# Linear attention and an MLP mixer on one core: head pairs, batched evacuations, weights cast by DMA, and the next batch's attention traced into each mixer

## The chip, the cores and the metric

The kernel runs on one core of a Trainium2 chip. A time is device microseconds (us) from launch to end, the median of several executions. The "span" in a profile runs from the first to the last instruction of one profiled execution and is some 2 us shorter. Engines are named as in the profile: PE (TensorE matmuls), PEld (TensorE weight loads), DVE (VectorE), ACT (ScalarE), POOL (GpSimd), SP (SyncE, which issues most transfers). An execution is called slow when it is over 1.5% above the fastest of the same kernel; only fast ones are compared.

## The reference, cut to what matters

Four batches, eight heads, 768 positions, head dimension 64. Retention attention carries a 64x64 state along the sequence; its output of all heads, side by side, is `x` (768 x 512) and goes through a two-stage mixer.

```python
# attention, per head h (gamma depends on h)
state = gamma * state + outer(k[t], v[t])
y[t]  = scale * q[t] @ state
# mixer, per batch
h  = relu(x.T @ w_tok1) @ w_tok2          # over positions: 768 -> 256 -> 768
u  = x + h.T
h2 = relu(u @ w_ch1) @ w_ch2              # over channels: 512 -> 1536 -> 512
out = u + h2
```

The recurrence is computed in six chunks of 128 positions: within a chunk a masked 128x128 score matrix, between chunks the state.

## The kernel before

All weights come first, as float32, and ACT casts them. Then 192 chunks (4 x 8 x 6) run one after the other, each with its own small loads, its own copies out of PSUM, and the state carried from chunk to chunk. The mixers follow in program order.

```python
for dst, src in ((w_tok1_sb, moe_w_tok1), ...):          # all weights first
    for i, t in enumerate(dst):
        nc.sync.dma_start(out=stg, in_=src[i * P:(i + 1) * P, :])
        nc.scalar.copy(t, stg)
for b in range(B):
    for h in range(H):
        for c in range(NC):
            ...                                          # three loads of 128 x 64
            nc.scalar.activation(qk16[:, :D], qk_sb[:, :D], AF.Copy, bias=0.0, scale=gt1p[h])
            nc.scalar.copy(k16, qk_sb[:, D:])
            nc.vector.tensor_scalar(vg16, v_sb, gk[h], None, ALU.mult)
            if c > 0:
                nc.scalar.copy(st16, st)
            nc.tensor.transpose(tp_ps, qk16, ident16)
            nc.scalar.copy(qgT, tp_ps[:D, :])
            nc.vector.tensor_copy(kT, tp_ps[D:, :])
            nc.tensor.matmul(a_ps, kT, qgT, start=True, stop=True)        # scores, 64 rows
            nc.vector.tensor_tensor(am_sb, a_ps, mask2[h], ALU.mult)
            nc.tensor.matmul(y_ps, am_sb, vg16, ...)
            nc.tensor.matmul(y_ps, qgT, st16, ...)
            nc.vector.tensor_copy(x_sb[b][c][:, h * D:(h + 1) * D], y_ps)
            nc.tensor.matmul(st_ps, k16, vg16, start=True, stop=True)
            nc.vector.tensor_scalar(st, st, g128[h], None, ALU.mult)
            nc.vector.tensor_tensor(st, st, st_ps, ALU.add)
# ... then, per batch, the mixer: 24 token matmuls of 512 columns, 24 transposes,
# 96 matmuls of 384 columns with w_ch1, 72 of 512 columns with w_ch2
```

## Time and profile before

| kernel before | value | where from |
|---|---|---|
| median time | 501.68 us (497.25 to 501.79, 3 runs) | times |
| span | 498.9 us | profile |
| first transpose, last transpose of attention | 21.0 and 446.7 us | the transposes' own list |
| PE, DVE, ACT, POOL busy | 75, 50, 56, 1% | first part of the page |
| mean granted clock | 0.832 | cores view |

The prediction below reads this profile part by part. The largest groups of instructions show many small ones. The columns are line, engine, operation, output and inputs, shapes and count, then busy time in us and the mean in ns, then the engine's idle time just before them and what ended most of it:

```profile
L120 ACT COPY qTt<-tp 64x128 f16<-64x128 f16 x192 | 49.7, 259 | 106.6 <-PE tp L117 103.1
L123 PE MATMUL p<-qTt,kTt 64*128 64x128 f16 x192 | 50.3, 262 | 38.5 <-DVE kTt L121 31.7
L125 DVE TENSOR_TENSOR am_sb<-p,dm 128x128 f16<-128x128 f32 x192 | 55.9, 291 | 45.3 <-PE p L123 36.3
```

Each of the three waits for another engine: that is the chain the prediction starts from.

### The profile page before, as it was taken

The numbers are of one execution on the slowest core, as the hardware profiler recorded it, in microseconds if no ns is written. First come the engines' busy times: TensorE is split into PE (matmuls) and PEld (weight loads), VectorE is DVE, ScalarE is ACT, GpSimd is POOL, SyncE is SP. The second block draws the span as 40 slices with busy tenths as digits, with TensorE's granted clock in tenths as the row PEclk, the third lists the DMA queues.
The fourth block names the chain that finished last, engine by engine and source line by source line (L and its number), as shares of the span: only waits on it lengthen the run. The fifth ranks groups of instructions, "written<-read, shape, count | busy, mean of one in ns | idle before, by whom it ended". The sixth has DMA issues, their size and how long they took to land.

```text
span 498.9 us, 7213 instructions
## 1 busy us (share of the span) xinstructions
PE 372.2 (75%) x1760; PEld 158.8 (32%) x1760; DVE 250.4 (50%) x1096; ACT 281.1 (56%) x1058; POOL 2.8 (1%) x15
## 2 busy tenths in 40 slices
PE   0034555547899999458999997568999998578997
PEld 0012222222344444222334433222344433222553
DVE  1035555555664566555744566554745566553012
ACT  6854444445787844456767744454677744456730
POOL 2000000000000000000000000000000000000000
PEclk9999999999957999655559998556758999557999
DMA  8832222222121232222211222222221233220002
GB/s 278 302 104 47 49 51 49 50 50 45 40 45 40 49 86 68 53 69 64 60 39 43 46 70 52 51 69 76 82 45 42 48 87 90 50 74 0 2 21 106
DMA packets 89899, 33.54 MB, mean 67 GB/s; under 512 B 83712, under 2 KB 84480, under 8 KB 89856
## 3 DMA queue, kind: packets, MB, share of 16 engines
q1 hardware_dynamic: 89856, 33.07, 25.1%
q8 instruction: 14, 0.23, 0.2%
q14 instruction: 29, 0.24, 0.2%
HBM read 26.74 MB, written 6.29 MB: 66 GB/s over the span
## 4 chain that ended last, share of the span: by engine, by line
PE 65%; DVE 14%; ACT 10%; DMA 5%; issue 5%; SPq 1%; ACTq 0%; DVEq 0%
PE acc L179 16%; PE acc L191 13%; PE p L123 8%; DVE am_sb L125 5%; PE p L131 5%; PE tp L117 5%; PE p L135 4%; PE p L130 4%; PE acc L152 4%; PE acc L162 3%; DVE kTt L121 3%; DMA wstg<-in_moe_w_ch_dram 3%; ACT qTt L120 3%; PE tp L173 2%; DVE x L132 2%
## 5 line engine op out<-in xcount | busy, mean ns | idle before, releaser
L120 ACT COPY qTt<-tp 64x128 f16<-64x128 f16 x192 | 49.7, 259 | 106.6 <-PE tp L117 103.1
L179 PE MATMUL acc<-uT,wc 128*128 128x384 f16 x384 | 95.2, 357 | 0.9 <-ACT h L185 0.4
L191 PE MATMUL acc<-wc,h 128*128 128x512 f16 x288 | 81.2, 389 | 0.1
L123 PE MATMUL p<-qTt,kTt 64*128 64x128 f16 x192 | 50.3, 262 | 38.5 <-DVE kTt L121 31.7
L125 DVE TENSOR_TENSOR am_sb<-p,dm 128x128 f16<-128x128 f32 x192 | 55.9, 291 | 45.3 <-PE p L123 36.3
L108 ACT ACTIVATE qk<-qk_sb,gt 128x64 f16<-128x64 f32 x192 | 66.5, 346 | 18.2 <-PE p L135 15.9
L132 DVE COPY x<-p 128x64 f32<-128x64 f32 x192 | 43.1, 225 | 66.0 <-PE p L131 54.5
L121 DVE COPY kTt<-tp 64x128 f16<-64x128 f16 x192 | 43.4, 226 | 48.5 <-ACT qTt L120 41.1
L117 PE MATMUL tp<-ident,qk 128*128 128x128 f16 x192 | 51.0, 266 | 22.4 <-ACT qk L110 22.1
L130 PE MATMUL p<-vg,am_sb 128*128 128x64 f16 x160 | 35.6, 222 | 29.3 <-DVE am_sb L125 29.2
L185 ACT ACTIVATE h<-acc 128x384 f16<-128x384 f32 x96 | 46.9, 489 | 17.9 <-PE acc L179 15.9
L111 DVE TENSOR_SCALAR vg<-v_sb,gk 128x64 f16<-128x64 f32 x192 | 46.9, 244 | 10.5 <-DMA v_sb<-in_v_dram 6.2
L123 PEld LDWEIGHTS <-kTt 64*128 64x128 f16 x192 | 18.7, 98 | 98.8 <-DVE kTt L121 80.6
L114 ACT CAST st<-state_sb 64x64 f16<-64x64 f32 x160 | 38.5, 241 | 17.5 <-DVE state_sb L140 15.3
L110 ACT CAST qk<-qk_sb 128x64 f16<-128x64 f32 x192 | 45.0, 234 | 0.9 <-DMA qk_sb<-in_k_dram 0.9
L135 PE MATMUL p<-vg,qk 128*64 128x64 f16 x160 | 35.3, 221 | 9.5 <-DVE x L132 4.7
L179 PEld LDWEIGHTS <-wc 128*128 128x128 f16 x384 | 33.2, 102 | 21.8 <-issue 6.9
L140 DVE TENSOR_TENSOR state_sb<-state_sb,p 64x64 f32<-64x64 f32 x128 | 27.3, 213 | 18.7 <-PE p L135 13.1
L131 PE MATMUL p<-st,qTt 64*128 64x64 f16 x160 | 34.9, 218 | 0.7 <-ACT st L114 0.6
L130 PEld LDWEIGHTS <-am_sb 128*128 128x128 f16 x160 | 16.7, 105 | 55.4 <-DVE am_sb L125 50.5
L198 DVE TENSOR_TENSOR o_sb<-x,acc 128x512 f32<-128x512 f32 x24 | 16.4, 685 | 35.6 <-PE acc L191 34.9
L135 PEld LDWEIGHTS <-qk 128*64 128x64 f16 x160 | 19.1, 120 | 44.0 <-issue 34.7
(35 smaller groups left out, 294.0 us busy)
## 6 DMA issues: line engine op xcount, KB each, us to landing
qk_sb<-in_q_dram SPq DMA_DIRECT2D x192, 32.0 KB, 1.7
qk_sb<-in_k_dram SPq DMA_DIRECT2D x192, 32.0 KB, 1.8
v_sb<-in_v_dram SPq DMA_DIRECT2D x192, 32.0 KB, 1.7
out_dram<-o_sb SPq DMA_DIRECT2D x24, 256.0 KB, 2.1
wstg<-in_moe_w_ch_dram SPq DMA_DIRECT2D x4, 768.0 KB, 8.8
wstg<-in_moe_w_ch_dram SPq DMA_DIRECT2D x12, 256.0 KB, 3.6
wstg<-in_moe_w_tok_dram SPq DMA_DIRECT2D x6, 128.0 KB, 2.3
wstg<-in_moe_w_tok_dram SPq DMA_DIRECT2D x2, 384.0 KB, 4.2
```

Source lines behind the costliest of these rows:

```text
L108: nc.scalar.activation(qk16[:, :D], qk_sb[:, :D], AF.Copy, bias=0.0, scale=gt1p[h])
L117: nc.tensor.transpose(tp_ps, qk16, ident16)
L120: nc.scalar.copy(qgT, tp_ps[:D, :])
L121: nc.vector.tensor_copy(kT, tp_ps[D:, :])
L123: nc.tensor.matmul(a_ps, kT, qgT, start=True, stop=True)
L125: nc.vector.tensor_tensor(am_sb, a_ps, mask2[h], ALU.mult)
L130: nc.tensor.matmul(y_ps, am_sb, vg16, start=True, stop=False)
L131: nc.tensor.matmul(y_ps, qgT, st16, start=False, stop=True)
L132: nc.vector.tensor_copy(x_sb[b][c][:, h * D:(h + 1) * D], y_ps)
L135: nc.tensor.matmul(st_ps, k16, vg16, start=True, stop=True)
L179: nc.tensor.matmul(h2_ps, w_ch1_sb[ct][:, ft * P:(ft + 1) * P], uT_sb[ct][:, sh * (S // 2):(sh + 1) * (S // 2)], start=(ct == 0), stop=(ct ...
L191: nc.tensor.matmul(o_ps, h2_sb[ft][:, i * P:(i + 1) * P], w_ch2_sb[ft], start=(ft == 0), stop=(ft == 11),)
```

## The change

Its intent: fewer and larger instructions beside the matmuls, no chain from chunk to chunk, no weight phase ahead of everything, and attention of batch b+1 laid among the mixer matmuls of batch b.

- Two heads share a tile of 128 partitions. Scores use 64 rows for each head; everything else uses the full array. The states of the two heads sit in a block-diagonal tile `R`, so one matmul reads both.
- The states of all chunks of a pair come from five matmuls and a short scan on DVE, not from a chain through the chunks. One copy empties three or six chunks.
- POOL casts k, scales the states and casts x and u to 16 bit.
- Weights are loaded by DMAs that POOL issues and that cast to 16 bit on the way, each issued behind the k cast of a pair.
- Attention is a generator of seven steps; the mixer loop advances it.

```diff
-            nc.sync.dma_start(out=stg, in_=src[i * P:(i + 1) * P, :])
-            nc.scalar.copy(t, stg)
+        if s == 0 and p == 2:
+            with tc.issue_after(kc.ins):
+                nc.gpsimd.dma_start(out=wc1, in_=moe_w_ch1.rearrange("(i p) j -> p i j", p=P))
...                                        # attention of one pair of heads
+        kc = nc.gpsimd.tensor_copy(k16..., kf...)            # 128 x 768
+        yield kc
+        for src, dst in ((q16, qT), (k16, kT)):
+            for c in range(NC):
+                nc.tensor.transpose(tp[:, c * P:(c + 1) * P], src[:, c]..., ident16)
+            nc.scalar.copy(dst, tp[:, :S])                   # six chunks at once
+        yield
+            for c in range(c0, c1):
+                nc.tensor.matmul(st[...], k16[:, c]..., v16[:, c]..., start=True, stop=True)
+            for c in range(c0, c1):                          # scan
+                    nc.vector.scalar_tensor_tensor(U[:, c], U[:, c - 1], gp[:, p:p + 1], s,
+                                                   ALU.mult, ALU.add)
+        for j in range(2):                                   # diagonal blocks of R
+            nc.gpsimd.tensor_scalar(R[r, :, r], U[r, :, r], g128[2 * p + j], None, ALU.mult)
+        yield
...                                        # scores and masks by three chunks, then y
+                    nc.tensor.matmul(o, qT[:, c * P:(c + 1) * P], R[:, c - 1], ...)
+                for j in range(2):
+                    nc.tensor.matmul(o[:, j * D:(j + 1) * D], ams[2 * hf + j][:, i], v16[:, c, j], ...)
+            nc.scalar.copy(xo, y...)
+            nc.gpsimd.tensor_copy(x16..., xo)
...                                        # the weave
+        for us in mlp(b):
+            spent += us
+            while steps and done < total and done < spent / MLP_US * total:
+                next(steps)                # one step of the next batch's attention
+                done += 1
```

## The prediction

> **What bounds the kernel now.** I read the busy shares first, then the table of busy time by stretches of 10 us, then the order of time of a single chunk, last the tail.
>
> ```profile
> PE 372.2 (75%) x1760; PEld 158.8 (32%) x1760; DVE 250.4 (50%) x1096; ACT 281.1 (56%) x1058; POOL 2.8 (1%) x15
> PE   0034555547899999458999997568999998578997
> ...
> PE 65%; DVE 14%; ACT 10%; DMA 5%; issue 5%; SPq 1%; ACTq 0%; DVEq 0%
> ```
>
> No engine is full. PE shows 75%, and 65% of the chain that ended last, but a matmul's recorded time is mostly its latency, so that row does not say PE is the limit. By stretches (start:end, length, then busy time and count of PE, PEld, DVE, ACT, POOL, granted clock, DMA share, GB/s):
>
> ```profile
> 10.00:20.00 10.00, 0.00 (x0) 0.00 (x0) 0.00 (x0) 9.73 (x23) 0.00 (x0) 1.00 0.87 342
> 60.00:70.00 10.00, 4.92 (x24) 2.33 (x23) 5.68 (x27) 4.50 (x21) 0.00 (x0) 1.00 0.22 48
> 170.00:180.00 10.00, 10.00 (x57) 4.38 (x58) 5.64 (x27) 6.46 (x25) 0.00 (x0) 1.00 0.23 52
> 210.00:220.00 10.00, 5.09 (x23) 2.46 (x23) 5.81 (x27) 4.58 (x22) 0.00 (x0) 0.50 0.20 44
> 470.00:480.00 10.00, 10.00 (x59) 5.47 (x57) 0.00 (x0) 7.07 (x15) 0.00 (x0) 1.00 0.00 0
> ```
>
> Until 20 us the core loads weights and ACT casts them; PE does nothing. In a stretch of attention alone (60 to 70) every engine is near half busy, which is the sign of a chain of waits. The mixer's dense matmuls (170 to 180) run *beside* attention, and DVE keeps its pace of 27 instructions per stretch: attention goes on at the same speed with or without the mixer. One chunk of one head in order of time:
>
> ```profile
> 63.90 0.29 PE L123 MATMUL p<-qTt,kTt 64*128 64x128 f16 x1 [0.36 <-DVE kTt L121]
> 64.23 0.29 DVE L125 TENSOR_TENSOR am_sb<-p,dm 128x128 f16<-128x128 f32 x1
> 64.58 0.23 PE L130 MATMUL p<-vg,am_sb 128*128 128x64 f16 x1 [0.39 <-DVE am_sb L125]
> 64.74 0.23 PE L131 MATMUL p<-st,qTt 64*128 64x64 f16 x1
> 65.01 0.23 DVE L132 COPY x<-p 128x64 f32<-128x64 f32 x1 [0.49 <-PE p L131]
> 65.80 0.29 PE L123 MATMUL p<-qTt,kTt 64*128 64x128 f16 x1 [0.61 <-DVE kTt L121]
> ```
>
> Scores wait for kT, the mask for scores, y for the mask: 1.9 us from one score matmul to the next. There are 192 chunks (4 batches, 8 heads, 6 chunks); their transposes (L117) run from 21.0 to 446.7 us, 2.2 us each. **So the time is 21 us of start, 192 x 2.2 = 426 us of attention chain, and a tail of 52 us in which the last mixer runs alone.** The first three mixers are already hidden. The tail shows what a mixer costs when fed:
>
> ```profile
> 465.72 14.05 PE L179 MATMUL acc<-uT,wc 128*128 128x384 f16 x80
> 479.61 15.70 PE L191 MATMUL acc<-wc,h 128*128 128x512 f16 x72
> ```
>
> That is 0.176 us per matmul of 384 columns and 0.218 of 512 at granted clock 1.00.
>
> **What the Trainium skill says.**
> 1. "TensorE: Matmul & The Clock Gate", Part 1: the array is at half clock until it has been densely busy for some 3.4 us, and falls back when idle. The trace agrees: clock 0.50 in attention alone, 1.00 in dense mixer stretches; the transpose of L117 is 289 ns at the median and 219 at the least. (For the first 130 us the record says 1.00 while the matmuls have the long durations; I take the clock as low there.)
> 2. "TensorEngine Tiling (Array Packing)", Key Properties: changing the tiling mode drains the array. In the warm stretch the start after a 64-row matmul (L123 at 164.56 us) came 0.16 us later, that after a full-row transpose (L117 at 165.63) 0.07 us later. The trace agrees in direction. The change keeps 64-row scores, so this stays to be paid.
> 3. "DMA: Bandwidth & Descriptors", Specifications and SWDGE vs HWDGE: under 512 B a transfer loses rate, and only GpSimd-issued DMAs can cast. Rows of q, k, v are 256 B: 48 GB/s at share 0.22 is about 218 GB/s flat out, against 342/0.87 = 393 for weights. The trace agrees on the first; no casting DMA is in it, so its rate is my largest unknown.
> 4. "GPSIMD Engine Reference", Engine selection: one-input elementwise on GpSimd is roughly line rate. The trace has only POOL's constants (297 ns for a 128x128 select), so no run shows it yet.
>
> **The change part by part.**
> *Pairs and batching.* 192 chunk chains become 16 head-pair units, each with six chunks per step, and states are computed ahead as a short scan rather than between chunks. What is left is work per engine. PE per pair: 12 transposes, 5 state products, 5 state reads, 12 y products on the full array, 34 x 0.07 = 2.4 us; 12 scores on 64 rows at about 0.14, 1.7 us; 4.1 us a pair, 16.4 us a batch. The row-tile pairs are issued one head after the other, so I give them no overlap.
> *Mixer on PE*, unchanged in matmuls: 24 x 0.218 + 96 x 0.176 + 72 x 0.218 + 24 transposes x 0.07 = 5.2 + 16.9 + 15.7 + 1.7 = 39.5 us. Together 56 us a batch at full clock.
> *DVE per batch.* Two rows give its line: 291 ns at 128 elements (L125), 685 at 512 (L198), so 160 + 1.03 N. Per pair: 4 scalings of 384 (0.56 each), 5 scan steps of 128 (0.29), 4 masks of 384 (0.56): 5.9 us; four pairs 24 and 12 adds of the mixer 8: 32 us.
> *ACT per batch.* 263 ns at 128 (L174) and 489 at 384 (L185), so 150 + 0.88 N: per pair two copies of 768 (0.83) and two of 384 (0.49), 2.6 us; four pairs 10.6, mixer (24 ReLUs at 0.49, eight evacuations at 0.60) 16.6: 27 us. Before it was 281/4 = 70.
> *POOL* takes k's cast, states to f16, x16 and u16: 26 instructions and 11,776 elements per partition a batch, at an estimated 1 to 2 ns each 17 to 29 us.
> So all three helpers have slack under PE's 56 us: **PE becomes the bound.**
> *Weights.* 7.9 MB no longer go first: 20 us of start (DMA and 17 us of ACT casts) leave. q, k, v of a batch are 4.7 MB, 21.6 us at 218 GB/s; the token weights (1.6 MB) and part of the rest share the engines with pairs 2 and 3. Weights at 393 GB/s are 20 us, next batch's q, k, v another 21.6, so about 63 us of DMA are queued from the start; the last weight (w_ch2) is needed when the first half's ReLUs are done, near 55 to 60.
> *Sum.* First batch's attention: 22 us of loads, about 6 of weights between them, then 8 us for the last pair's chain (cast, transpose, evacuate, mask, y, x16): 36 us. Three batches of mixer with attention woven in: 56 each plus waits. I put the waits at 7 us each: 2 at the batch boundary (last y to ACT to POOL to the first token matmul), 4 in the second token stage (each of 6 tiles goes PE, DVE, POOL, PE, ACT, some 2.5 us of latency with two buffers), 1 for accumulators waiting behind ACT's long copies. 3 x 63 = 189. Last mixer alone: 39.5 and 4 to 5 of the same waits and the last store: 44. 36 + 189 + 44 = 269; I say **268 us**, a ratio of 0.53.
>
> **The rivals.**
> *A. Near-perfect weave.* The scheduler fills the token stage with attention, waits fall to 2 us each, start 30: 30 + 174 + 41 = 245. For it: in the kernel before, mixer and attention already interleave matmul by matmul and PE is recorded as busy throughout 160 to 190.
> *B. Casting DMA or GpSimd too slow.* If casts move at half of 393 GB/s, the weights take 40 us of all engines, w_ch2 lands near 80 and the first mixer waits some 20 us: 290. If POOL needs 3 ns an element, its 37 us still fit, but the token stage waits twice as long and the clock drops: 3 x 6 more, 286. Nothing before speaks for or against, as POOL was 1% busy.
> *C. The clock stays at 0.50 through the woven stages*, as it did from 210 to 260. Mixer 39.5 would be near 75 and the total beyond 400. Against it: dense stretches such as 170 to 180 were at 1.00 with attention beside them.
> *D. Transfers limit.* 25 MB of q, k, v, out at 218 to 393 GB/s are under 110 us in all: hidden after the start.
>
> **Range and chances.** A and B are the likely sides, A at a quarter, B at a third, C at 3%. Range 242 to 297. Even C would be faster than 501.68, so over 2% faster has 0.98; 0.01 each is for an error I don't see.
>
> **What would show it right or wrong.** Right: the mixer's matmul rows keep 0.16 to 0.22 us spacing, PE is at its own pace in four stretches of some 60 us, clock near 1.00 after the first 40 us; first token matmul near 36 us; ACT, DVE, POOL near 110, 125, 80 us in sum. Wrong: PE idle in the token stage on u16 (POOL) beyond 6 us a batch; PE idle waiting for w_ch1 or w_ch2 by DMA; 64-row scores costing much more than 0.14 us; clock 0.50 inside woven stages; ACT copies of 768 holding the accumulators, seen as matmuls waiting for the ReLU.

## The result, and the profile after

| | before | after |
|---|---|---|
| median, beside each other on one chip | 499.47 us (496.89 to 501.79, 4 runs) | 256.28 us (255.64 to 256.81, 4 runs) |
| span | 498.9 us | 253.9 us |
| mean granted clock of the profiled run | 0.832 | 0.987 |
| PE, DVE, ACT, POOL busy in sum (us) | 372, 250, 281, 3 | 215, 112, 103, 83 |

The ratio is 0.5119, with a 95% interval of 0.5089 to 0.5149. It is worked out from fast runs and is not quite the quotient of the medians above (0.5131). The time fell inside the predicted range, 12 us below the point. All outputs were correct.

The page of the changed kernel, its busy shares, the same rows by 40 slices of 6.3 us, and the chain that ended last:

```profile
PE 214.7 (85%) x1600; PEld 120.1 (47%) x1600; DVE 112.5 (44%) x275; ACT 103.3 (41%) x195; POOL 82.8 (33%) x119
...
PE   1564557759999998969999989789999988999994
...
PEclk9999999997999999999999999979999999999999
DMA  8999999999808996998541012000010021002112
...
PE 60%; DVE 13%; DMA 9%; POOL 8%; issue 4%; ACT 4%; SPq 1%; POOLq 0%; DVEq 0%; ACTq 0%
...
PE acc L220 23%; PE acc L228 22%; DMA vf<-in_v_dram 6%; POOL r L160 6%; DVE am L171 4%; DVE x L206 3%; DVE U L156 3%; PE acc L196 3%; PE a L169 3%; DMA qf<-in_q_dram 2%; PE tp L138 2%; PE yp L180 2%; PE yp L182 2%; POOL u L208 1%; DVE q L124 1%
```

Read the PE row in two parts. For nine slices, until 57 us, PE is half busy, and the DMA row stands at 9; from the tenth on PE is near 9, and it stays there when the DMA row falls to 0 to 2 after 21 slices. So transfers may hold the beginning but not the rest. The chain agrees: the two large mixer products (L220, L228) are now 45% of it. Stretches of time (start:end, length, then PE, PEld, DVE, ACT, POOL busy with counts, granted clock, DMA share, GB/s; the DMA share adds up the time of packets, so packets that overlap can bring it over 1):

```profile
0.00:40.00 40.00, 20.02 (x173) 14.02 (x174) 21.29 (x73) 10.94 (x17) 18.99 (x31) 1.00 1.22 212
40.00:70.00 30.00, 23.88 (x173) 13.55 (x171) 13.82 (x33) 13.71 (x27) 13.15 (x20) 0.94 1.08 203
70.00:115.00 45.00, 41.61 (x339) 22.67 (x336) 25.01 (x57) 18.47 (x37) 17.14 (x24) 1.00 0.82 176
115.00:160.00 45.00, 43.45 (x344) 24.37 (x345) 21.40 (x50) 21.42 (x41) 13.48 (x19) 1.00 0.31 80
```

The starts of the first token matmul (L196, the first thing that a mixer does) cut the span into stages: 43.5, 101.4, 154.8, 209.0 us and the end at 253.9. So the first batch's attention takes **43.5 us**, the three woven stages **57.8, 53.4 and 54.2**, the last mixer **44.9**.

What one pair costs on PE in a woven stage can be read from the order of time (start, length, engine, line, operation, count, and in brackets the idle time before and what ended it):

```profile
103.94 0.50 PE L138 MATMUL tp<-ident,q 128*128 128x128 f16 x6
104.27 0.50 PE L138 MATMUL tp<-ident,k 128*128 128x128 f16 x6
...
106.18 0.35 PE L169 MATMUL a<-qT,kT 64*128 64x128 f16 x6 [0.27 <-ACT kT L140]
...
106.46 0.61 PE L204 MATMUL acc<-h,wt 128*128 128x512 f16 x2
...
113.15 0.22 PE L180 MATMUL yp<-r,qT 128*128 128x128 f16 x1
...
113.20 0.22 PE L182 MATMUL yp<-v,am 128*128 128x64 f16 x2
...
113.26 0.22 PE L180 MATMUL yp<-r,qT 128*128 128x128 f16 x1
```

A line's length ends with the latency of its last matmul, so the pace is read from start to start. Six transposes take 104.27 - 103.94 = 0.33 us, 0.055 each. Six score products of 64 rows are followed by the next matmul after 0.28 us, so they are no slower. (At 122.84 us in the same trace six more stand between mixer matmuls with no idle time before them; the next starts after 0.28 us too.) One state read and two y products take 0.11 us, 0.055 + 2 x 0.03. A pair is then 12 transposes, 5 state products, 5 state reads and 12 scores at 0.055 plus 12 y products at 0.03: 1.9 + 0.4 = some 2.2 us.

The first 43 us look different. The states' scaling on POOL marks the pairs:

```profile
13.61 2.21 POOL L160 TENSOR_SCALAR r<-U 64x320 f16<-64x320 f32 x2
...
20.36 2.08 POOL L160 TENSOR_SCALAR r<-U 64x320 f16<-64x320 f32 x2 [2.75 <-DVE U L156]
...
29.77 2.09 POOL L160 TENSOR_SCALAR r<-U 64x320 f16<-64x320 f32 x2 [4.69 <-DVE U L156]
...
31.92 0.51 POOL L186 CAST x<-x 128x384 f16<-128x384 f32 x1
...
32.38 0.83 POOL L126 CAST k<-kf 128x768 f16<-128x768 f32 x1
...
39.39 2.12 POOL L160 TENSOR_SCALAR r<-U 64x320 f16<-64x320 f32 x2 [4.64 <-DVE U L156]
```

The second pair follows the first after 6.8 us, the third and fourth after 9.4 and 9.6. In this trace that is not a wait for loads: from 11.7 us, when k of the second pair is in, to the first token matmul, no engine's wait is ended by one. POOL stands twice in the circle: it scales one pair's states for 2.1 us, casts that pair's x, and only then casts the next pair's k, whose transposes, states and scan (4.6 us of waiting) lead back to POOL.

Last, the transfers. SP's loads and the weights share the DMA engines. A load of 384 KB that takes SP some 1.75 us to issue elsewhere took 8.2 us (at 24.8) and 7.4 us (at 40.0) while a channel weight was on its way (w_ch1 was issued at 23.7 us, w_ch2 at 33.1). The last line shows DVE idle for v of the next batch's first pair, which SP had issued at 33.1:

```profile
10.72 1.75 SPq L106 DMA_DIRECT2D kf<-in_k_dram  x1
...
39.95 7.36 SPq L106 DMA_DIRECT2D kf<-in_k_dram  x1
...
48.73 0.75 DVE L130 TENSOR_SCALAR v<-vf,gv 128x384 f16<-128x384 f32 x2 [9.18 <-DMA vf<-in_v_dram]
```

### The profile page after: what moved, and what is told of

The parts are those of the page before. It is cut to its first block, busy times and chain, and to the rows that moved or that the text cites. A ratio compares the mean times of both kernels' runs of the same rounds, so it can differ in the third digit from the quotient of the medians.

```text
span 253.9 us, 4101 instructions
## 1 busy us (share of the span) xinstructions
PE 214.7 (85%) x1600; PEld 120.1 (47%) x1600; DVE 112.5 (44%) x275; ACT 103.3 (41%) x195; POOL 82.8 (33%) x119
## 4 chain that ended last, share of the span: by engine, by line
PE 60%; DVE 13%; DMA 9%; POOL 8%; issue 4%; ACT 4%; SPq 1%; POOLq 0%; DVEq 0%; ACTq 0%
PE acc L220 23%; PE acc L228 22%; DMA vf<-in_v_dram 6%; POOL r L160 6%; DVE am L171 4%; DVE x L206 3%; DVE U L156 3%; PE acc L196 3%; PE a L169 3%; DMA qf<-in_q_dram 2%; PE tp L138 2%; PE yp L180 2%; PE yp L182 2%; POOL u L208 1%; DVE q L124 1%
## 5 line engine op out<-in xcount | busy, mean ns | idle before, releaser
L220 PE MATMUL acc<-uT,wc 128*128 128x384 f16 x384 | 72.6, 328 | 0.8 <-ACT h L223 0.5
L228 PE MATMUL acc<-wc,h 128*128 128x512 f16 x288 | 68.0, 380 | 0.0
L220 PEld LDWEIGHTS <-wc 128*128 128x128 f16 x384 | 35.7, 98 | 25.3 <-issue 4.9
L160 POOL TENSOR_SCALAR r<-U 64x320 f16<-64x320 f32 x32 | 32.3, 1009 | 38.8 <-DVE U L156 37.2
L171 DVE TENSOR_TENSOR am<-a,mask 128x384 f16<-128x384 f32 x64 | 34.3, 553 | 13.2 <-PE a L169 12.8
L228 PEld LDWEIGHTS <-h 128*128 128x128 f16 x288 | 26.2, 98 | 27.3
L233 DVE TENSOR_TENSOR o<-x,acc 128x512 f32<-128x512 f32 x24 | 16.5, 686 | 49.4 <-PE acc L228 49.4
L185 ACT COPY x<-yp 128x384 f32<-128x384 f32 x32 | 15.1, 479 | 47.8 <-PE yp L182 47.8
L180 PE MATMUL yp<-r,qT 128*128 128x128 f16 x80 | 14.7, 243 | 13.6 <-POOL r L160 10.3
L186 POOL CAST x<-x 128x384 f16<-128x384 f32 x32 | 16.9, 527 | 28.1 <-ACT x L185 27.9
L156 DVE SCALAR_TENSOR_TENSOR U<-U,gp,yp 128x128 f32<-128x128 f32 x64 | 21.9, 343 | 1.1
L169 PE MATMUL a<-qT,kT 64*128 64x128 f16 x192 | 17.0, 240 | 4.5 <-ACT kT L140 2.4
L208 POOL CAST u<-x 128x512 f16<-128x512 f32 x24 | 14.6, 624 | 18.6 <-DVE x L206 18.5
L182 PE MATMUL yp<-v,am 128*128 128x64 f16 x192 | 18.9, 213 | 0.0
L206 DVE TENSOR_TENSOR x<-x,acc 128x512 f32<-128x512 f32 x24 | 16.0, 683 | 5.6 <-PE acc L204 5.2
## 6 DMA issues: line engine op xcount, KB each, us to landing
wc<-in_moe_w_ch_dram POOLq DMA_DIRECT2D x2, 1536.0 KB, 13.8
```

The lines of the kernel that those rows point to most:

```text
L156: nc.vector.scalar_tensor_tensor(U[:, c], U[:, c - 1], gp[:, p:p + 1], s, ALU.mult, ALU.add)
L160: nc.gpsimd.tensor_scalar(R[r, :, r], U[r, :, r], g128[2 * p + j], None, ALU.mult)
L169: nc.tensor.matmul(a[:, i], kT[r, t], qT[r, t], start=True, stop=True)
L171: nc.vector.tensor_tensor(am, a, mask, ALU.mult)
L180: nc.tensor.matmul(o, qT[:, c * P:(c + 1) * P], R[:, c - 1], start=True, stop=False)
L182: nc.tensor.matmul(o[:, j * D:(j + 1) * D], ams[2 * hf + j][:, i], v16[:, c, j], start=(c == 0), stop=(c == 0 or j == 1))
```

## The experiments

Each run is correct unless said otherwise, and was timed beside the kernel before, not beside the change, and on several chips (medians of the kernel before: 499.4 to 503.1 us). "Ratio" is against the kernel before; 0.5119 is the change's own. Where two intervals of ratios overlap, a difference in total of 1 or 2 us is not clear of noise. The stages of the traces are firmer: the last mixer took 44.9 to 45.1 us in every fast profile but one (not woven, 45.7). "Starts" are those of the first token matmul of the four batches; the change's are 43.5, 101.4, 154.8, 209.0.

### 1. What the weave is worth

```diff
-            while steps and done < total and done < spent / MLP_US * total:
-                next(steps)
-                done += 1
+            pass                           # all of it is traced after the mixer
```

> One part undone: the next batch's attention is traced after the whole mixer, not between its steps. The changed kernel took 256.3 us. Theory (PE is the bound in the three woven stages, 53 to 58 us each, and the weave is what keeps it fed): the four attentions become stretches of a latency chain as the first one is (9.4 us per pair, PE half idle), so three times 15 to 25 us come back: 300 to 330 us. Rival (the scheduler fills the gaps by itself, as it did in the kernel before, so the hand-made weave adds little): 250 to 268 us.

Measured: 305.53 us, ratio 0.6109 (0.6072 to 0.6146). Starts 43.6, 116.8, 188.0, 257.9. Two stretches, one within a mixer, one of attention alone (columns as above):

```profile
64.00:90.00 26.00, 25.56 (x137) 12.83 (x136) 4.29 (x7) 7.73 (x16) 0.00 (x0) 1.00 0.61 134
90.00:117.00 27.00, 15.81 (x172) 11.22 (x172) 18.76 (x47) 9.07 (x16) 13.21 (x18) 0.67 0.86 164
```

The theory holds. Attention alone takes some 27 us a batch with PE busy for 16 of it and the clock down to 0.67; woven, its matmuls cost PE some 9 us. The weave is worth 305.5 - 256.3 = **49 us**. The rest, 499 to 306, belongs to pairs, batching and the weights' new place together.

### 2. Weights: held back, or not cast by DMA

First, w_ch2's load was moved from behind the first batch's fourth k cast to behind the next batch's first:

```diff
-        if s == 0 and p == 3:
-            with tc.issue_after(kc.ins):
-                nc.gpsimd.dma_start(out=wc2, ...)
+                kc = next(steps); done += 1             # in the weave
+                if b == 0 and done == 1:
+                    with tc.issue_after(kc.ins):
+                        nc.gpsimd.dma_start(out=wc2, ...)
```

> The casting load of w_ch2 is issued only after the k cast of the next batch's first pair. In the changed kernel DVE waited 9.2 us for v of that pair, which landed at 48.7 us behind w_ch2, with the first mixer's additions queued behind it. Theory (the first mixer is held by that order of transfers): v lands near 37 to 40 us, the wait of DVE goes, the second batch's first token matmul comes 5 to 9 us sooner than at 101.5, total 247 to 251. Rival (all transfers together bound the first 70 us, the order doesn't matter): w_ch2 or later pairs come late instead, total within 1% of 256.3.

Measured: 254.33 us, ratio 0.5086. Starts 47.8, 98.6, 152.6, 206.9. The v that had come at 48.7 now came at 41.1, with a wait of 1.5 us in place of 9.2:

```profile
41.14 1.23 DVE L130 TENSOR_SCALAR v<-vf,gv 128x384 f16<-128x384 f32 x2 [1.50 <-DMA vf<-in_v_dram]
```

The theory had the cause of that wait right, and its worth wrong: the second batch starts 2.8 us sooner, but the first token matmul 4.3 us *later*. In the trace the next batch's state products and scores, free to run now that v is there, stand in PE's order before it (43.7 to 47.2 us). Of the 9.2 us on DVE some 2 reach the end, and even these are not clear of noise (0.5049 to 0.5122, against 0.5089 to 0.5149).

Second, the weights went back to plain float32 loads by SP and casts on ACT, in the same places:

```diff
-                nc.gpsimd.dma_start(out=wc1, in_=moe_w_ch1.rearrange("(i p) j -> p i j", p=P))
+            staged(moe_w_ch1, wc1, 1)     # per slice: nc.sync.dma_start(out=stg, ...);
+                                          #            nc.scalar.copy(wc1[:, i:i + 1], stg)
```

> One part undone: weights as f32 through SP's queue and cast on ACT (some 15 us of ACT), traced at the same places. Theory (ACT has slack, and the casting DMA only saves ACT work that was off the path; in SP's one queue the weights can't crowd out q, k, v): total 250 to 262 us. Rival (ACT's casts sit in the chain of the first attention, as they did in the kernel before where ACT was busy with them until 20 us): 265 to 280 us.

Measured: 264.67 us, ratio 0.5287, clock 0.961. Starts 42.8, 109.7, 163.8, 218.0. It lies between the two theories. SP issues in order, and the eight slices of the channel weights stand ahead of the next batch's q. Each slice takes only 0.3 to 0.5 us to issue, but the eight are spread over 28.6 us, because they go through four staging tiles that ACT's casts have to empty. The last two lines are from the list of SP's own waits (total, times, longest):

```profile
22.50 28.58 SPq L105 DMA_DIRECT2D wstg<-in_moe_w_ch_dram  x8
...
60.68 0.82 PE L146 MATMUL tp<-ident,q 128*128 128x128 f16 x6 [8.82 <-DVE q L132]
...
SPq L105 <- ACT wt L106: 14.1, 2, 9.5
SPq L105 <- ACT wc L106: 7.8, 4, 2.9
```

So the casting loads are worth some 8 us here, nearly all of it in the stage from 42.8 to 109.7, where q came late. ACT has its part in that: its casts stood in order behind its copies for the first batch (the first at 34.6 us), and SP, and so q, waited for them. More staging tiles were not tried, so how much a second queue is worth by itself is not shown. One thing the run does show: without casting loads no load of q, k or v took over 10.0 us from issue to landing; in the change the longest took 16.1.

### 3. Whose turn it is on POOL, ACT and DVE

k's cast on ACT, to take POOL out of the circle of the first batch once:

```diff
-        kc = nc.gpsimd.tensor_copy(k16..., kf...)
+        nc.scalar.copy(k16..., kf...)     # weights then anchored behind POOL's R of pairs 0, 1, 2
```

> k's cast moves from GpSimd to ACT, weights keep their place after GpSimd's state scaling. In the changed kernel each pair's k cast stood behind the previous pair's state scaling and x16 cast on GpSimd, and pairs of the first batch followed each other every 9.4 us. Theory (that order on GpSimd is what made the first attention 43.5 us, not the transfers): pairs follow at 6 to 8 us, the first token matmul comes at 34 to 39 us; of the gain some is lost to the wait for v of the next batch, total 246 to 254. Rival (first attention is bound by its transfers): first token matmul stays at 42 to 44 us, total within 1% of 256.3.

Measured: 259.87 us, ratio 0.5197; starts 49.9, 105.6, 159.1, 213.2. The theory falls as a total, and half of it stands; the rival falls too (49.9 is not 42 to 44). States were scaled at 13.9, 20.7 and 29.2 us, but the fourth pair's only at 44.8:

```profile
44.00 0.42 DVE L124 TENSOR_SCALAR q<-qf,gq 128x384 f16<-128x384 f32 x1 [6.93 <-DMA qf<-in_q_dram]
...
44.84 2.12 POOL L160 TENSOR_SCALAR r<-U 64x320 f16<-64x320 f32 x2 [10.49 <-DVE U L156]
```

In DVE's order the *next batch's* q scaling stood ahead of the last scan step of the fourth pair. An engine runs its instructions in order, so a load that came late for batch 1 held up batch 0.

Half of the states' scaling on ACT:

```diff
-            nc.gpsimd.tensor_scalar(R[r, :, r], U[r, :, r], g128[2 * p + j], None, ALU.mult)
+            if j == 0: nc.gpsimd.tensor_scalar(R[r, :, r], U[r, :, r], g128[2 * p + j], None, ALU.mult)
+            else:      nc.scalar.activation(R[r, :, r], U[r, :, r], AF.Copy, bias=0.0, scale=g128[2 * p + j])
```

> The state scaling of the second head of each pair goes to ACT (estimate from ACT's rows: 0.15 + 320 x 0.00088 = 0.43 us), that of the first stays on GpSimd (1.01 us). In the changed kernel PE waited 10.3 us for GpSimd's scaling in all, and the two scalings are 2.1 us of each pair's chain. Theory: the pairs of the first batch follow at 8.4 instead of 9.4 us and PE's wait in the second token stages halves: total 248 to 253 us. Rival (the chain then waits for something else that ended just before, or ACT's queue puts the scaling behind an evacuation): within 1% of 256.3.

Measured: 252.90 us, ratio 0.5064; starts 49.7, 102.1, 154.2, 206.3. The total is in the theory's range, but only one of its two sources held: the woven stages fell to 52.4, 52.1 and 52.1, while the first batch got longer. Its first three pairs did follow faster (states at 13.7, 19.6 and 27.4 us). But the weights are issued behind the k casts of these pairs, so they went out sooner too (w_ch1 at 21.8, w_ch2 at 29.6 us, not 23.7 and 33.1), and v of the fourth pair, issued at 19.7, was 22.2 us on its way:

```profile
42.03 0.75 DVE L130 TENSOR_SCALAR v<-vf,gv 128x384 f16<-128x384 f32 x2 [14.29 <-DMA vf<-in_v_dram]
```

Both halves on DVE, together with w_ch2 held back:

```diff
-            nc.gpsimd.tensor_scalar(R[r, :, r], U[r, :, r], g128[2 * p + j], None, ALU.mult)
+            nc.vector.tensor_scalar(R[r, :, r], U[r, :, r], g128[2 * p + j], None, ALU.mult)
```

> Both state scalings on DVE (an estimate from DVE's two rows: 0.3 to 0.5 us each, against 1.01 on GpSimd), where they follow the scan that feeds them, and w_ch2 held as in hold_wc2. r_split gave 252.9 us by shortening the woven stages to 52.1 us, hold_wc2 254.3 by the second batch's start at 98.6. Theory (the two gains are of different stages and add): second batch's first token matmul at 97 to 100, the two woven stages at 51 to 52.5 us each, total 247 to 251 us, the best version so far. Rival (DVE's extra 10 us of work delays the mixer's additions and masks in the token stages, or the first stage is bound by transfers whatever the order): 252 to 257.

Measured: **248.44 us** (248.22 to 251.19, 4 runs), ratio 0.4956 (0.4924 to 0.4987); starts 47.1, 97.8, 149.7, 201.7. The theory holds. This is the best version found and beats both kernels: 3.1% below the change. DVE does a pair's two scalings in 0.7 us in most places where POOL took 2.1, and PE no longer waits for POOL at the state reads (10.3 us in the change; 1.0 us for DVE here). The scaling on DVE was not run without the weight held back.

### 4. Is the first batch bound by order, by small pieces, or by both

Pairs of the first batch started every two steps in place of four, with four attention buffers (with two, the build stops in a deadlock of the schedule, so there is no such run):

```diff
-    order = sorted((4 * p + s, s, p) for p in range(NP) for s in range(NS))
+    order = sorted((2 * p + s, s, p) for p in range(NP) for s in range(NS))
```

> First batch only: a pair starts two steps after the one before it instead of four, with four buffers instead of two for its tiles. In the changed kernel pairs of the first batch follow every 9.4 us with PE half idle; moving k's cast alone did not cure it (8.5 us and then a wait for the next batch's loads). Theory (the start is a latency chain of pairs that overlap too little): first token matmul at 34 to 39 us instead of 43.5; but v of the next batch still lands near 48 us behind the weights, so DVE's wait of 9 us grows to 12 to 16 and total stays at 251 to 257. Rival (loads bound the first attention): first token matmul at 41 to 44.

> The same as stagger2, and the weights wait: token weights after the third pair's k cast, w_ch1 after the fourth's, w_ch2 after the next batch's first. Theory (two things bound the first 100 us, the overlap of the pairs and weights crowding out q, k, v; taken away together they give what neither gives alone): first token matmul at 34 to 38 us, second batch's at 90 to 95 instead of 101.4, total 244 to 249 us. Rival (the sum of the transfers bounds the first 70 us, whatever the order): second batch's first token matmul at 98 to 101, total 253 to 257.

Measured: 257.04 us, ratio 0.5149, starts 47.4, 103.1, 156.7, 210.8; and, with every weight one pair later besides, 257.26 us, ratio 0.5154, starts 45.1, 102.3, 157.5, 210.9. Both theories fall on the first start, and the second run ends near its rival's total of 253 to 257 (its second start, 102.3, lies beyond the rival's 98 to 101). In the first, w_ch1 went out at 18.1 us in place of 23.7, and DVE waited 6.1 us for a q, until 32.0. In the second the fourth v came in time (scaled at 28.8 us, after a wait of 0.2), but that pair's chain ran on to 42.3 us, and the next batch's first pair stood in PE's order ahead of the token matmuls.

Loads in pieces of 1.5 KB in place of 256 B. The positions are permuted by this, so **the result is wrong**; shapes, instructions and bytes stay:

```diff
-                out=t, in_=src[b, 2 * p:2 * p + 2].rearrange("h (c p) d -> p (h c) d", p=P))
+                out=t.rearrange("p (h c) d -> p h c d", h=2),
+                in_=src[b, 2 * p:2 * p + 2].rearrange("h (p c) d -> p h c d", p=P))
```

> A wrong result on purpose: q, k and v are loaded with six consecutive positions on each partition, so that each contiguous piece is 1.5 KB instead of 256 B; bytes, instructions and waits are the same, the positions are permuted. It measures what the small pieces cost. Theory (the first 62 us are bound by transfers of 256 B pieces, at about 220 GB/s): the loads of the first batch are in by 14 to 18 us instead of 25 to 29, v of the next batch no longer holds DVE, second batch's first token matmul at 84 to 93 instead of 101.4, total 240 to 249 us. Rival (the first 62 us are the latency chain of four pairs): first token matmul still at 40 to 44 us, total 252 to 257.

Measured: 258.12 us, ratio 0.5130; starts 50.0, 103.2, 157.4, 211.5. The theory falls, and the rival's first start (40 to 44) too. The page's row of GB/s by slice, and a wait:

```profile
GB/s 197 375 326 268 240 260 268 332 273 44 95 91 197 114 123 135 136 102 61 125 95 92 0 41 84 0 0 3 0 82 43 1 86 41 0 3 82 41 41 82
```
```profile
40.28 0.75 DVE L124 TENSOR_SCALAR q<-qf,gq 128x384 f16<-128x384 f32 x2 [7.65 <-DMA qf<-in_q_dram]
```

The loads did get faster, 375 GB/s in the second slice where the change shows 218, and the transfers of the beginning are over by 58 us. Nothing was gained. With the first loads done sooner, k is cast sooner and so the channel weights are issued sooner (14.4 and 21.6 us, not 23.7 and 33.1), beside the loads still to come; a weight's load took 24.5 us from issue to landing in place of 13.8. So faster loads alone do not shorten the first stages while the weights follow them. What they would bring with the weights held back was not tried.

Last, the best version with two changes that act only ahead of the second stage: each weight one pair later, and the weave begun 3 us of mixer work later in the first mixer.

```diff
-        if s == 0 and p == 1:              # token weights; w_ch1 likewise from 2 to 3
+        if s == 0 and p == 2:
...
+        late = 3.0 if b == 0 else 0.0
-            while steps and done < total and done < spent / MLP_US * total:
+            while steps and done < total and done < (spent - late) / (MLP_US - late) * total:
```

> The best version so far (states scaled on VectorE, w_ch2 held back: 248.44 us, first token matmul at 47.1, second at 97.8) with two more changes that act only before the second stage: each weight's load is issued one pair later, and the first mixer begins to weave the next batch's attention 3 us of mixer work later, so that in PE's order only the five state products of the next batch's first pair, not its transposes and scores, stand between the last y product and the first token matmul. In the best version v of the first batch's fourth pair was waited for 4.96 us and scaled at 36.06, and the next batch's transposes stood among the last y products. Theory (late loads and foreign work in PE's order are what stretches the first batch's end): that v is scaled before 32 us, the first token matmul starts at 39 to 43 us, the second at 92 to 96, the later stages stay at 52, total 242 to 246. Rival (the first 98 us are bound by the sum of their transfers and fillers, so that what is taken from the first stage comes back in the second): first token matmul earlier by 2 to 5 us but the second still at 96 to 100, total 247 to 251.

Measured: 254.16 us, ratio 0.5059 (0.5027 to 0.5091); starts 39.0, 103.4, 155.4, 207.4. The order of time, from the end of the first batch (v of its fourth pair, first line) into the stage after it:

```profile
31.54 0.74 DVE L130 TENSOR_SCALAR v<-vf,gv 128x384 f16<-128x384 f32 x2
...
33.57 14.64 SPq L106 DMA_DIRECT2D vf<-in_v_dram  x1
...
38.97 4.53 PE L196 MATMUL acc<-x,wt 128*128 128x512 f16 x12 [0.24 <-POOL x L186]
...
48.46 0.42 DVE L124 TENSOR_SCALAR q<-qf,gq 128x384 f16<-128x384 f32 x1 [8.57 <-DMA qf<-in_q_dram]
...
54.63 0.75 DVE L130 TENSOR_SCALAR v<-vf,gv 128x384 f16<-128x384 f32 x2 [4.53 <-DMA vf<-in_v_dram]
...
55.29 1.28 DVE L206 TENSOR_TENSOR x<-x,acc 128x512 f32<-128x512 f32 x2
...
56.02 1.01 PE L204 MATMUL acc<-h,wt 128*128 128x512 f16 x2 [11.03 <-DVE x L206]
```

The first half of the theory holds, for the changes together: without late loads and with less foreign work in the order, the first batch's attention is done at **39.0 us**, 8 us sooner than in the best version. The second half falls, and the rival was too mild: the first woven stage took 64.5 us in place of 50.6. The two channel weights now moved together with the next batch's loads. One issue of SP lasted 14.6 us. DVE stood 8.6 us at a q of the next batch and 4.5 at a v, and behind these in DVE's order stood the *mixer's* own additions (L206), for which PE then waited 11 us. What the first stage won, the second gave back with interest.

### 5. Two small parts, each taken back

Scores of the two heads issued in turn, not one head after the other:

```diff
-            for j in range(2):
-                for i in range(HC):
+            for i in range(HC):
+                for j in range(2):         # two score tiles open at once
```

> The score products alternate between the two heads (rows 0 to 63, then rows 64 to 127) instead of three of one head and then three of the other. In the trace of the changed kernel they already follow each other every 0.055 us at full clock, as full-row matmuls of 128 columns do, where the prediction took 0.14. Theory (the 64-row products cost no more than full-row ones, there is little left to gain): total 254 to 258 us, within 1% of 256.3. Rival (row tiles of one head in a row lose the overlap that two heads would have, 12 x 0.028 us in each of 16 pairs): 5 us less, 250 to 252.

Measured: the median of its fast runs lies at 257 us (256.66 to 257.17), ratio 0.5146 (0.5122 to 0.5170). There is nothing in it, as expected.

Copies and masks for one chunk at a time, as before the change:

```diff
-            nc.scalar.copy(dst, tp[:, :S])
+            for c in range(NC):
+                nc.scalar.copy(dst[:, c * P:(c + 1) * P], tp[:, c * P:(c + 1) * P])
...                                        # masks and y copies likewise
```

> One part undone: masks, the evacuations of q and k transposed and of y are done chunk by chunk (128 columns) as before the change, not three or six chunks at once. From the rows of 128 and 384 elements: DVE 12 x 0.29 instead of 4 x 0.55 per pair, 1.3 us more; ACT 12 x 0.26 and 6 x 0.26 instead of 2 x 0.80 and 2 x 0.48, 2.1 us more; 16 pairs, so DVE 133 and ACT 137 us in all, both still far below PE. Theory (fixed costs of small operations are off the path in the woven stages, where PE is the bound): woven stages 53 to 55 us, start 3 to 5 us later, total 256 to 264 us. Rival (batching is what made the change fast, by shortening each pair's chain): woven stages beyond 57 us, total over 270.

Measured: 260.99 us, ratio 0.5185 (0.5157 to 0.5212); starts 48.2, 105.4, 159.9, 214.5. Woven stages of 57.1, 54.6 and 54.6 in place of 57.8, 53.4 and 54.2: the fixed costs of small copies lie on ACT and DVE, which have room beside PE, and it is the first batch, a chain, that pays 4.7 us for them. The theory holds.

## Why the prediction was right, and where its terms were off

The prediction's sum was 36 + 3 x 63 + 44 = 269. The trace has 43.5 + (57.8 + 53.4 + 54.2) + 44.9 = 253.8. The mechanism was right; two terms were mis-sized with opposite signs, 7.5 us too little (the start) and 23.6 us too much (the woven stages, of which 3 x 7.5 = 22.5 us is attention on PE). The first hid a third of the second, and that is luck: with the start alone put right the sum would have been 276.

- **"PE becomes the bound"**: confirmed. PE 85%, 8 or 9 in nearly every slice after 60 us, clock 0.97 to 1.00 over each woven stage; of the second stage's 53.4 us, 39.5 + 8.9 = 48.4 are matmuls at their own pace. Without the weave, clock and PE share fall (experiment 1).
- **Mixer 39.5 us**: right. Eight products with w_ch2 took 1.90 us from the first start to the last end. Less one latency of 0.38 that is 0.217 each, against the 0.218 taken from the tail before.
- **Attention on PE, 4.1 us a pair and 16.4 us a batch**: the step that failed most. It measured 2.2 and 9. I had taken 0.07 us for a full-array product and 0.14 for a 64-row score from the spacing in the kernel before, where each small product stood alone between mixer matmuls. In rows of six they cost 0.055, 64-row scores included. The Trainium skill, "TensorE: Matmul & The Clock Gate", Back-to-back issue gap, gives N/2.4 + 2.5 ns, 56 ns at 128 columns, as the gap of what it calls isolated products on a warm array; the trace agrees with 0.33 us for six. Only the trace says so: for a stream of weight load and product the same section gives some 81 ns, which would have left the term near the predicted one (an estimate: 46 x 0.081 = 3.7 us a pair). Experiment 5 shows that the order of the heads has nothing to add.
- **Waits of 7 us a stage**: 53.4 - 39.5 - 8.9 = 5.0 in the second woven stage. The first had 9.4, with DVE 9.2 us idle for v of the next batch, and the third 5.8: 20.2 in all against 21, so this term was right. (Holding w_ch2 back took the first stage to 50.8 us, but 4.3 of the 7.0 us moved into the start.)
- **Start, 36 us**: 43.5. I took loads as the pace (5.4 us a pair) and added one last chain. Measured, loads were waited for only until 11.7 us; then each pair was a chain of up to 9.6 us that includes POOL twice. Yet a shorter chain alone did not help: in three runs that shortened it (k on ACT, half of the states on ACT, pairs two steps apart) the weights went out behind it at other times, a load then came late (waits of 6.9, 14.3 and 6.1 us), and the start was 47.4 to 49.9 us. Only with states off POOL, weights later and less foreign work in PE's order, all together, did it take 39.0 us.
- **Helpers 110, 125, 80 us** for ACT, DVE, POOL: 103, 112, 83. (One sum is not what it says: 11,776 elements at 1 to 2 ns are 12 to 24 us, so POOL's 17 to 29 has some 5 us more in it; at 3 ns, rival B's 37 would then be near 41.)
- **Rival A (245 us)**: the change does not reach it, but 248.4 with the states on DVE comes close, and its "start 30" was not seen in any run. **Rival B** was half true: a casting load of 3.1 MB took 13.8 us from issue to landing, near 230 GB/s of source, under the 393 of plain weights. But q, k and v shared the engines in that time, so this is no rate of the cast by itself. And w_ch2 was not waited for: it was issued at 33.1, so at that pace landed near 47, and its first use was at 71.4. The harm was to q, k and v beside it. **Rival C** is out. **Rival D** was called hidden after the start; transfers in fact reach into the second stage.

What stays open is a single cause for the first 100 us. The woven kernels run here moved the first mixer's start between 39.0 and 50.0 us and the second's between 97.8 and 109.7, and the earliest first start went with a late second. Late loads, POOL's turns and the next batch's work ahead in an in-order engine were each shown to hold an engine; none taken away alone was worth more than 3.4 us at the end, and faster loads alone brought nothing. The runs fit two limits that lie close together, the chain of the pairs and the transfers, so that shortening one brings out the other; no run takes both away. A version that keeps the 39.0 us start and the 50.6 us stage was not found.

## What to carry to other kernels

Where small products come in rows on a warm array, count them at the pace of such a row (0.055 us here), not at the spacing of lone ones. A circle of waits that passes twice through one slow engine shows where a chain can be shortened; before you count the gain, ask what is issued behind its steps. Here that was the weights, which then went out sooner and held up the loads. Where one batch's work is woven into another's, a late load of the *next* batch can hold the present one, since each engine runs in order: time the issue of transfers against what stands behind them in the order, and look at the stage after before calling an earlier start a gain. The state scaling on VectorE, with the last weight held back, is the version to keep here: 248.4 us.

## What the Trainium skill lacked or had wrong

- "TensorE: Matmul & The Clock Gate", Back-to-back issue gap: its sustained figures for streams of weight load and matmul, some 81 ns at 128 columns and 131 ns at 512, do not fit. The runs show 55 ns (six transposes, each with a weight load, in 0.33 us) and 217 ns (512 columns, each with a weight load). The formula in the same section for what it calls the isolated gap fits both.
- "TensorEngine Tiling (Array Packing)", Key Properties: it says that a change of mode drains the array but not how little that is in rows: six 64-row scores with full-row products before and after them, and no idle time, took 0.28 us (122.84 to 123.12), so here the drain was not to be seen. Its independent tiles gave nothing when two heads took turns (ratio 0.5146 against 0.5119).
- "DMA: Bandwidth & Descriptors": no rate for casting transfers, and no figure for how much a load on one queue holds up another queue's. A casting load with 3.1 MB of source took 13.8 us from issue to landing beside loads of q, k and v; SP's issue of a 384 KB load beside it lasted 7.4 us in place of 1.75, once 14.6; and a load of 384 KB took up to 22.2 us to land (experiment 3), where none took over 10.0 without casting loads.
- "GPSIMD Engine Reference", Engine selection: "1-input is roughly line-rate" held for no scaling here. 64x320 elements took POOL 1009 ns; DVE did two of them in 0.7 us. A cast of 128x768 took POOL 834 ns, so the phrase fits the casts (DVE would need some 0.95 us for 768 elements, an estimate by the prediction's line from DVE's two rows), but the scaling of fewer than half as many elements a partition cost more than the cast.
- "TensorE: Matmul & The Clock Gate", Seeing it yourself: it ties a clock of 13/16 to three busy cores of a die. Here a program on one core had one run of 297.32 us at a mean granted clock of 0.791, where the same kernel's other runs took 257 at 0.98 to 0.99; what else ran on the die is not in the trace, and no page says how to meet this with one core.
